# ReLU²-attention followed by a two-layer GELU block: a fourth batch's first layer in block form behind attention, and a new order of all operations

## The chip, the cores and the metric

One core of a Trainium2 chip. The time is the device time of one execution in microseconds (us); lower is better. Engines: PE (TensorE, matmuls), DVE (VectorE), ACT (ScalarE), POOL (GpSimd, which here mainly issues loads), SP (SyncE, which issues transposing transfers and stores).

## What is computed

Eight batches, twelve heads, 448 tokens, head size 64. All inputs and the output are float32; the kernel computes in bf16 with float32 sums.

```python
scores = (q @ k.T) / sqrt(64)                  # per batch and head
attn   = maximum(scores, 0)**2 / 448
x      = (attn @ v), heads side by side        # (8*448) x 768
h      = x @ w_in                              # 768 -> 2048
out    = gelu_exact(h) @ w_out                 # 2048 -> 768
```

## The kernel before

**Attention.** Batches 0 and 1 are transposed on PE. From batch 2 on, `add_load` issues one load for each four heads ("group") of k and q from POOL, casting to bf16, and one load `ldV` for a whole batch of v. `add_T_dma` then issues nine transposing transfers from SP (`turn`, L662): per group one for k (`kT`) and an even and an odd one for q (`qT`). A batch's q and k lie in one buffer, `nq` and `nk`, that all batches from 2 on share: a group of the next batch can only be loaded when this batch's transpositions of it are done. `add_gate` (L703) is a tiny POOL copy that reads a transposed tile; everything behind it in POOL's queue, the next loads above all, waits until that group's transpositions have landed. `qT` and `kT` have two buffers each, so batch b's transpositions also wait for the scores of batch b-2.

Per batch there are 21 score steps (`QK`, L736, four quadrant matmuls), each followed by a ReLU that empties PSUM (ACT L748 or DVE L750) and a square on DVE (L757), and three value products (`AV`, L797, 28 matmuls each) whose results are copied to `xT`.

**First layer.** In plain form (`add_f1`, L849) a batch takes 16 products of six matmuls of 448 columns, each followed by a GELU on ACT. In block form (`add_blocks`, `add_block`, L993) x and `w_in` are cut in 2x2 blocks and seven products of half-size blocks replace eight: 28 products of six matmuls of 224 columns, plus four sums of x blocks (L960), and, for each of four sub-blocks, one copy out of PSUM on ACT and five additions on DVE (L1030). The sums of weight blocks (`add_wsums`, L918) are made once; one of them overwrites a part of `win_sb`, so no plain product may come after it. Batches 0 to 4 are plain, batches 5 to 7 in block form.

**Second layer.** Tokens are taken in groups of 256 (`add_group`, L1166), seven products each, with sums and additions on DVE (L1147, L1200) and two stores from SP (L1127) out of three `osb` buffers. The first 256 tokens are done by `add_plain` (L1261).

**Order.** Every operation is an `Op` in one list, `sch.open`. `Scheduler.place` walks a string, `ORDER`, and issues the operations in that order: a letter names the engine (P PE, A ACT, D DVE, G POOL, S SP), the number is the operation's place in the list. `Z1056` is a filler: matmuls on zeros of 1056 columns (L1499). Each engine runs its own operations strictly in this order, so an operation that waits holds up all behind it on its engine. Between the attention steps PE runs "flow": plain first-layer products and second-layer groups; what belongs to `end` follows.

Of the kernel before, what the change touches and what calls it, by code (L numbers as in the profile page):

```python
# [26 lines left out]
KF = FF // 128  # L27
# [24 lines left out]
LEAD = 8  # L52
HALF_M = 6
# [30 lines left out]
G0 G1 G2 G3 G1435 G4 G5 G6 A10 P11 D13 A16 P17 G7 D12 P14 D18 P42 P39 G8 P19 A15 P21 D43 P33 P36 D44  # L84
A40 D20 Z128 A22 P54 G9 P25 P23 A37 D34 P51 D26 P48 A55 Z1056 D35 A24 P69 D56 Z1024 D41 A49
P57 Z992 D38 A52 P63 Z448 G117 D70 P45 A58 D53 P66 A64 D50 P27 A46 G118 P31 D59 P60 D28 A67
G119 D32 A47 P78 P29 D65 G120 A61 P81 Z1088 D68 D30 A79 P93 D62 P108 Z544 D71 A82 P84 Z992
G121 A94 P75 D109 P72 G122 D83 A85 P90 P129 D80 G123 D73 A76 P105 A74 P102 D95 G124 P131 D130
A91 P141 D86 A106 D77 P111 P96 D132 A103 P165 P143 D92 A112 D104 D107 A97 P156 D113 P87 G125
D98 A166 P99 D110 G126 D88 A157 P114 A142 D100 A89 P174 G127 A101 P168 D115 P133 A144 P135  # L90
A116 G128 D175 P171 P159 A169 D134 P251 D136 D170 A160 P145 D158 A172 D167 A252 P162 P186 D176
P192 P243 A146 D161 G147 D173 A187 G148 P253 D193 A163 A244 D164 P195 G149 P180 P198 P137 A254
G150 P139 D196 A181 P183 P177 G151 D138 A199 D140 A184 P189 P219 P245 D178 G152 A190 D185 P247
G153 D194 A220 D179 A246 G154 P213 D188 P222 P204 P263 D221 A248 G155 D197 A214 D200 P265 D191
A205 D182 A264 P261 A223 A266 P216 D224 S231 P207 P201 D206 A262 A208 S229 P210 P259 D209 A217
D215 S232 P255 D211 A260 P249 D212 D218 A256 D202 P225 A203 S228 A250 P257 S230 A226 P267 D227
A258 P348 S234 A268 P350 S233 A349 P352 G237 A351 G238 P354 S235 A353 G239 P288 S236 P294 P282
P358 A355 G240 G241 D289 P356 D283 A359 P360 D295 A357 D290 P306 P279 P276 D296 P362 A361 D307
P364 D280 A363 P366 D277 A365 P368 A367 P370 A369 P300 P285 P291 G242 P372 A371 G269 D286 A292
P374 G270 D284 A373 G271 P318 P303 D301 P312 G272 P376 D308 A375 G273 A304 D319 P378 D278 A377  # L100
P380 D313 A379 D293 G274 D314 D390 P382 D305 G275 D302 A381 D391 D287 D281 P330 P309 P297 S398
D392 A331 D320 P315 S399 P384 D393 A298 D396 A310 S401 A383 D417 P387 D394 D419 A385 D311 A299
D395 A316 D317 P324 P321 D418 A325 P333 D397 P327 A388 P421 D420 D322 S400 A328 D323 P423 D326
A334 D422 S386 P339 P336 P342 P425 D424 D329 A343 D335 P427 S402 A426 D337 P429 G407 A340 G408
S403 D428 P431 G409 D344 D338 S389 D341 P440 P437 D332 P345 S404 D430 A438 P443 D441 P446 S405
P433 D432 A346 D347 A444 P509 A447 D434 P511 D439 G410 D448 S406 A510 G411 P449 D442 P452 G412
P455 P513 D562 A512 S435 D445 S436 A453 P515 D454 A450 A514 P517 D456 D451 P464 D457 P461 P458
S541 A465 P467 D462 A518 P470 G413 S542 P519 A516 G414 A459 G415 P521 D471 S543 G416 D472 A520
P523 D466 A468 D460 S544 A522 P479 D560 P476 P473 D469 P525 A524 D463 A477 P527 D480 A474 D478
A526 P529 D475 D481 A528 P488 P485 P482 S545 A489 P494 D486 A530 P491 P531 D487 D483 P533 D495  # L110
A532 S546 P535 D496 A484 D561 A492 P503 D490 P500 A534 P497 D493 P537 A536 G550 G551 S547 P564
D498 G552 A538 D504 S548 P539 D499 A501 G553 A565 D505 P600 G554 D502 P603 P506 G555 S549 A601
P606 D604 A540 P609 P566 D563 A507 D602 P568 D607 D567 P570 D610 A569 A508 P572 D571 P624 P612
P618 S704 P574 D580 D608 A613 D573 P576 S705 G556 A619 D581 G557 D582 P627 S706 D575 P615 G558
P584 D614 G559 D577 S578 A616 D611 P586 S707 D605 A628 D617 A625 P636 D620 P630 S579 A585 P621
D629 G713 A631 D637 P633 G714 P588 D587 S708 G715 A622 D626 D623 A634 P639 P642 P648 D583 P590
D638 A640 D635 A589 D632 P592 D641 A643 D591 P651 A649 S709 D644 P657 P645 D593 A652 P666 D658
P654 P594 D653 A646 D659 A655 D650 P596 A647 D667 S710 D595 P660 P766 P663 P672 D597 A661 D767
P674 A664 S711 D662 A673 D656 P676 D668 A675 D665 P772 P769 P669 S712 G716 D773 A770 P763 S598
P775 A677 G717 P678 S599 D670 G718 A764 D771 P680 G719 D723 A776 S867 D768 A679 P790 P778 D765  # L120
A671 P781 G720 P682 A681 D777 G721 D791 P684 G722 S868 D725 A683 P686 D779 A782 A685 P688 D783
D780 D774 P787 P793 P784 D724 S869 A788 P799 D794 A687 P796 P690 A689 D795 D789 A797 P692 D798
A691 P694 A693 P696 A785 A695 S870 P698 A786 A800 P802 P811 A697 P805 D801 P700 A699 A803 D812
P702 S871 D792 A806 D804 P814 P817 D807 P808 A815 S872 P823 D818 A701 P820 P727 G876 D816 A703
G877 D809 S873 A821 G878 D726 P729 A810 D819 A728 D822 P826 D813 A824 P829 S874 P906 P731 D730
G879 A830 G880 D827 S875 P733 G881 A907 D828 D831 P912 D825 P921 P832 D745 A913 P909 A732 D922
P924 P735 D734 A833 A925 P737 A910 D743 A834 P936 D914 P918 P933 D736 P739 D738 S741 D744 A934
P747 D908 G882 A937 D740 G883 P749 D938 A919 S978 G884 D935 A748 G885 D926 P942 P930 S742 P915
P751 D750 A931 D943 S979 P753 D920 A916 A752 D746 P755 D923 S980 D911 D944 P948 P945 D917 P927
D888 A949 D754 P939 P757 D950 A928 D886 D756 P759 A946 D887 A940 D758 A929 P835 D932 D947 D941  # L130
S981 P957 P954 P951 A836 D958 A955 P960 P963 D760 P837 D959 A961 D952 P839 D956 A953 S982 A838
P966 D964 P972 P969 D962 P841 A840 S983 D889 A973 D965 P843 S984 A842 D967 P847 A970 S985 A844
P845 D971 D968 S761 D974 P990 P987 D1067 P975 S986 A991 P993 D988 A846 P996 S762 P849 D992
A848 D1068 A976 D1070 P851 A997 D989 A850 P853 A994 A977 D995 P1005 P1002 A852 P999 P855 A854
D1006 A1003 P859 D1004 A1000 D998 A856 P857 D1007 D1001 P1011 P1014 P1008 D1059 A858 A1012
P1017 D1015 P1026 P861 A1009 D1063 A860 P863 D1060 A1018 D1010 P1020 A1027 P1029 D1061 P1023
A862 P865 D1016 A864 D1019 P890 A1021 D1028 D1022 A866 P892 D1062 A1024 A891 D1013 P894 D1025
A1030 D1069 D893 P1035 D1031 P1038 P1032 D1064 A895 A1036 D1066 P1041 D1037 A1039 P1044 P896
D1033 A1042 D1034 D1040 P898 A1045 D1043 D897 P1047 D1046 P1050 P1053 P900 D899 A1048 D1139
P902 D1049 A1051 D1140 A1054 P1071 D1052 D1055 P1056 D901 S904 A1072 D903 S905 P1088 D1141  # L140
P1073 D1057 P1090 A1089 D1058 P1143 D1074 D1091 P1075 D1065 P1092 A1144 P1077 D1142 A1076
D1179 P1094 A1093 D1180 P1079 D1078 P1096 D1095 P1145 D1080 D1097 A1081 P1082 D1181 A1098
P1099 D1146 P1085 D1083 P1102 D1100 A1084 P1105 D1086 A1101 P1122 D1103 A1087 P1107 D1182
A1106 P1124 A1123 P1147 A1104 D1108 D1125 P1109 P1126 A1148 P1111 A1110 P1128 A1127 P1113
D1112 P1130 D1129 P1149 D1114 D1131 A1115 P1116 A1132 P1133 D1150 P1119 D1117 P1136 D1134
A1118 P1151 D1120 A1135 D1137 A1121 P1153 D1291 A1138 D1292 D1152 P1155 D1159 D1154 S1157
P1163 D1160 D1156 S1158 P1165 D1161 D1164 P1167 D1162 D1166 D1293 P1169 D1294 A1168 P1171
D1170 P1173 D1253 D1172 P1175 D1251 D1174 S1177 P1183 D1252 P1200 D1176 S1178 P1185 A1184
D1254 P1202 A1201 P1255 D1186 D1203 P1187 P1204 A1256 P1189 A1188 P1206 A1205 P1191 D1190
P1208 D1207 P1257 D1192 D1209 A1193 P1194 A1210 P1211 D1258 P1197 D1195 P1214 D1212 A1196  # L150
P1217 D1198 A1213 P1234 D1215 A1199 P1219 A1218 P1236 A1235 P1259 A1216 D1220 D1237 P1221
P1238 A1260 P1223 A1222 P1240 A1239 P1225 D1224 P1242 D1241 P1261 D1226 D1243 A1227 P1228
A1244 P1245 D1262 P1231 D1229 P1248 D1246 A1230 P1263 D1232 A1247 D1249 A1233 P1265 A1250
D1264 P1267 D1271 D1266 S1269 P1275 D1272 D1268 S1270 P1277 D1273 D1276 P1279 D1274 D1278
P1281 D1280 P1283 D1282 P1285 D1365 D1284 P1287 D1363 D1286 S1289 P1295 D1364 P1312 D1288
S1290 P1297 A1296 D1366 P1314 A1313 P1367 D1298 D1315 P1299 P1316 A1368 P1301 A1300 P1318
# [240 lines left out]
def kernel(  # L397
# [537 lines left out]
    def add_blocks(b):  # L935
# [34 lines left out]
        for m4 in (0, M1 // 2):  # L970
# [4 lines left out]
            for p in zip(*todo):  # L975
                atoms += [(0.58, o) for o in p]
# [445 lines left out]
    def at(b, n):  # L1422
        return [at_slot(b, n)]
# [112 lines left out]
```

## Time and profile before

| | |
|---|---|
| three runs, median (lowest, highest) | 370.13 us (369.83, 370.37) |
| profiled execution, first to last instruction (span) | 367.9 us |
| PE busy | 359.3 us, 98% |
| DVE, ACT, POOL busy | 285.1 (78%), 199.4 (54%), 62.9 (17%) us |
| HBM read, written | 45.61 MB, 11.01 MB |
| score steps of batch 7 on PE | 220.5 to 246.5 us |

The profiled execution has no other time than its span. The span goes from the first to the last instruction; the 2.2 us between it and the median lie around it, and are taken as the same before and after. "Busy" of PE is modelled, since matmuls overlap; how many microseconds a group of matmuls takes is read from the start of one group to the start of the next.

### The profile page before, as it was taken

What the parts mean: (1) busy time and instruction counts of PE and PEld (TensorE: products, weight loads), DVE (VectorE), ACT (ScalarE), POOL (GpSimd) and SP (SyncE); (2) the same over time, 40 slices, a digit from 0 to 9 for tenths busy, and PEclk for the clock granted to TensorE, in tenths of its full rate; (3) what the DMA queues carried; (4) which work ended last, traced back from release to release, by engine and by line L of the source; (5) the groups of instructions that cost most, each with busy time, mean ns of one, the idle gap of its engine ahead of it and who ended that gap; (6) DMA issues with size and microseconds to landing.
All of it is one profiled execution on the core that took longest, in us unless ns stands there. A gap on an engine that the chain in (4) does not pass through costs nothing.

```text
span 367.9 us, 8474 instructions
## 1 busy us (share of the span) xinstructions
PE 359.3 (98%) x3573; PEld 222.5 (60%) x3573; DVE 285.1 (78%) x473; ACT 199.4 (54%) x319; POOL 62.9 (17%) x103
## 2 busy tenths in 40 slices
PE   7999999999999999999999999999999999999995
PEld 6675654455544455544555544557876897688663
DVE  4998854699788889989598997998788558665862
ACT  5998954536367546765777568863540353045200
POOL 8766304230112140240302000000000000000000
PEclk9999999999999999999999999999999999999998
DMA  9999999999999999999999980002002301210233
GB/s 180 191 202 204 201 178 167 196 201 178 162 218 214 154 186 193 237 214 154 166 110 131 215 183 2 2 2 86 3 0 87 88 0 52 86 37 2 86 87 86
DMA packets 89542, 47.27 MB, mean 128 GB/s; under 512 B 55329, under 2 KB 86049, under 8 KB 89505
## 3 DMA queue, kind: packets, MB, share of 16 engines
q0 software_dynamic: 32912, 22.47, 43.8%
q1 hardware_dynamic: 55952, 23.76, 34.9%
q8 instruction: 28, 0.46, 0.5%
q10 hardware_dynamic: 640, 0.51, 0.4%
q14 instruction: 10, 0.07, 0.1%
HBM read 45.61 MB, written 11.01 MB: 154 GB/s over the span
## 4 chain that ended last, share of the span: by engine, by line
PE 78%; DMA 8%; SPq 5%; DVE 5%; issue 1%; POOL 1%; ACT 1%; DVEq 0%; POOLq 0%; ACTq 0%
PE pso L1166 30%; PE psh L849 19%; PE pb L993 13%; PE ps L736 8%; PE pav L797 7%; SPq L662 5%; DMA wout_sb<-in_moe_w_out_dram 4%; DVE a_sq L757 2%; DMA nq<-in_q_dram 1%; DVE t_sb L1103 1%; DMA qT<-nq 1%; DMA out_dram<-osb 1%; ACT a_sq L748 1%; PE tp L635 1%; DVE part L1030 1%
## 5 line engine op out<-in xcount | busy, mean ns | idle before, releaser
L748 ACT ACTIVATE a_sq<-ps 128x896 bf16<-128x896 f32 (+1 forms) x119 | 104.3, 918 | 36.8 <-PE ps L736 36.6
L757 DVE TENSOR_TENSOR a_sq<-a_sq 128x896 bf16<-128x896 bf16 (+1 forms) x169 | 97.0, 617 | 9.4 <-ACT a_sq L748 8.8
L849 PE MATMUL psh<-xT,win_sb 128*128 128x448 bf16 (+1 forms) x516 | 96.4, 340 | 0.4 <-issue 0.4
L849 PEld LDWEIGHTS <-win_sb 128*128 128x128 bf16 x516 | 48.1, 98 | 45.8 <-issue 9.7
L750 DVE TENSOR_SCALAR a_sq<-ps 128x896 bf16<-128x896 f32 (+1 forms) x50 | 53.5, 1078 | 17.1 <-PE ps L736 17.0
L859 ACT ACTIVATE h_sb<-psh 128x448 bf16<-128x448 f32 x80 | 43.2, 548 | 29.9 <-PE psh L849 29.6
L1166 PEld LDWEIGHTS <-s_sb 128*128 128x128 bf16 x424 | 40.7, 98 | 26.6 <-issue 2.0
L1030 DVE TENSOR_TENSOR part<-pb,part 128x448 f32<-128x448 f32 x60 | 34.6, 620 | 21.5 <-PE pb L993 21.5
L736 PE MATMUL ps<-qT,kT 64*64 64x448 bf16 (+1 forms) x756 | 47.9, 336 | 0.5 <-ACT a_sq L748 0.2
L1166 PEld LDWEIGHTS <-h_sb 128*128 128x128 bf16 x312 | 29.6, 98 | 22.5 <-issue 4.4
L1166 PE MATMUL pso<-wout_sb,s_sb 128*128 128x384 bf16 (+2 forms) x216 | 38.1, 320 | 0.1
L1166 PE MATMUL pso<-wout_sb,h_sb 128*128 128x384 bf16 x208 | 38.1, 326 | 0.0
L1166 PE MATMUL pso<-t_sb,s_sb 128*128 128x384 bf16 x208 | 38.1, 326 | 0.0
L797 PE MATMUL pav<-a_sq,v_sb 64*64 64x448 bf16 (+1 forms) x756 | 36.5, 329 | 0.3 <-issue 0.2
L736 PEld LDWEIGHTS <-kT 64*64 64x64 bf16 x756 | 18.5, 105 | 22.9 <-issue 17.1
L1039 ACT ACTIVATE h_sb<-part 128x448 bf16<-128x448 f32 x36 | 20.1, 578 | 20.2 <-DVE part L1030 19.9
L1200 DVE TENSOR_TENSOR osb<-pso,p_sb 128x384 f32<-128x384 f32 x39 | 21.7, 556 | 11.0 <-PE pso L1166 6.7
L993 PEld LDWEIGHTS <-win_sb 128*128 128x128 bf16 x288 | 27.6, 98 | 2.3 <-issue 0.4
L797 PEld LDWEIGHTS <-v_sb 64*64 64x64 bf16 x756 | 21.2, 107 | 11.7 <-issue 1.3
L703 POOL COPY gate<-qT 128x16 bf16<-128x16 bf16 x15 | 3.7, 246 | 111.0 <-DMA qT<-nq 111.0
L993 PEld LDWEIGHTS <-ws 128*128 128x128 bf16 x216 | 20.7, 98 | 0.0
L1147 DVE TENSOR_TENSOR s_sb<-h_sb 128x1024 bf16<-128x1024 bf16 x26 | 17.8, 685 | 2.3 <-PE pso L1166 2.3
(61 smaller groups left out, 298.4 us busy)
## 6 DMA issues: line engine op xcount, KB each, us to landing
nk<-in_k_dram POOLq DMA_DIRECT2D x23, 224.0 KB, 5.6
nq<-in_q_dram POOLq DMA_DIRECT2D x21, 224.0 KB, 8.3
v_sb<-in_v_dram POOLq DMA_DIRECT2D x5, 672.0 KB, 13.9
out_dram<-osb SPq DMA_DIRECT2D x8, 336.0 KB, 2.9
v_sb<-in_v_dram POOLq DMA_DIRECT2D x9, 224.0 KB, 8.6
out_dram<-osb SPq DMA_DIRECT2D x7, 288.0 KB, 3.2
out_dram<-osb SPq DMA_DIRECT2D x8, 240.0 KB, 3.0
win_sb<-in_moe_w_in_dram POOLq DMA_DIRECT2D x8, 192.0 KB, 8.6
```

Source lines behind the costliest of these rows:

```text
L736: nc.tensor.matmul(ps[64 * j : 64 * j + 64, e, x * w : x * w + w], kT[r, g, i * 128 + 64 * j : i * 128 + 64 * j + 64], moving, start=True, ...
L748: A.activation(ar, ps, AF.Relu, scale=c_att)
L750: V.tensor_scalar(ar, ps, c_att, 0.0, op0=mybir.AluOpType.mult, op1=mybir.AluOpType.max,)
L757: V.tensor_mul(box["a2"][:, :, :used], ar, ar)
L797: nc.tensor.matmul(pav[0][o2 : o2 + 64, e, :w], vt[b][r, 2 * g + e, bass.ts(i, D)], box["a2"][r, y, o : o + w], start=(i == 0), stop=(i == ...
L849: nc.tensor.matmul(ph[:, x * n : x * n + n], win_sb[:, kd, bass.ts(m + x, 128)], xT[b][:, kd, c], start=(kd == 0), stop=(kd == KD - 1),)
L859: A.activation(h_ring()[:, m : m + nm, o + c.start : o + c.stop], box[0][:, :S].rearrange("p (x n) -> p x n", x=nm), AF.Gelu,)
L993: nc.tensor.matmul(bank[name][:, y, z * HS : z * HS + HS], w[:, k, bass.ts(mm, 128)], right()[:, k], start=first and k == 0 and z == 0, st ...
L1030: V.tensor_add(get(to), ps(name), get(other))
L1039: A.activation(h_ring()[:, m : m + 2, o + half[c].start : o + half[c].stop], src().rearrange("p (x n) -> p x n", x=2), AF.Gelu,)
L1166: nc.tensor.matmul(box[bank][:, n0:n1], left()[:, kf], right()[:, kf, n0:n1], start=bool(need) and kf == 0, stop=kf == K2 - 1, skip_group_ ...
L1200: V.tensor_add(out()[:, n0:n1], box[bank][:, n0:n1], other()[:, n0:n1])
```

## The change

Batch 4 joins the batches in block form, so its 16 plain products leave attention's flow and 28 block products come behind it. The second-layer group 6 moves from batch 5's flow to batch 4's. Tiles for the x-block sums are dealt out differently (batch 6 takes the `qT` buffer, batch 7 waits for batch 4's products). `ORDER` is replaced as a whole; it has 1469 operations instead of 1436.

```diff
+NBLK = 4
 ...
-G0 G1 G2 G3 G1435 G4 G5 G6 A10 P11 D13 A16 P17 G7 D12 P14 D18 P42 P39 G8 P19 A15 P21 D43 P33 P36 D44
-A40 D20 Z128 A22 P54 G9 P25 P23 A37 D34 P51 D26 P48 A55 Z1056 D35 A24 P69 D56 Z1024 D41 A49
 ...
+G3 G4 G1468 G1 G0 G7 G118 A10 P11 D13 G117 A16 P17 D12 P14 G2 D18 P42 P39 G122 P25 D15 P23 A43
+G6 P33 D26 P36 A40 P21 G5 D24 P69 P19 A34 G9 P66 D37 P63 D22 A70 Z1216 D20 P57 A67 P48 D41 P29
 ...
@@ add_blocks
-                    tag = "qT" if b == B - 1 else "kT"
+                    tag = "qT" if b == B - 2 else "kT"
 ...
-        gone = [o for (bb, *_), o in QK.items() if bb == (B - 2 if b == B - 3 else B - 1)]
+        gone = [o for (bb, *_), o in QK.items() if bb == (B - 2 if b == B - NBLK else B - 1)]
+        if b == B - 1:
+            gone += first_blocks
 ...
-    F1B = {2: 1, 3: 2, 4: 3, 5: 4}
-    GROUPS = {2: (1,), 3: (2, 3), 4: (4, 5), 5: (6,)}
+    F1B = {2: 1, 3: 2, 4: 3}
+    GROUPS = {2: (1,), 3: (2, 3), 4: (4, 5, 6)}
 ...
-    add_wsums(at(B - 1, 1), [F1[B - 4, m, None] for m in range(KF)])
+    add_wsums(at(B - 1, 1), [F1[B - NBLK - 1, m, None] for m in range(KF)])
 ...
-    end = woven(add_blocks(B - 3), add_group(7))
+    end = add_blocks(B - 4)
+    end += woven(add_blocks(B - 3), add_group(7))
```

The two `ORDER` strings are too long to print. Counted out by the list of operations, they say this (K4.1: load of k, batch 4, group 1; V4: v of batch 4; kT, qE, qO: the transpositions of k, and the even and odd ones of q):

| | before | after |
|---|---|---|
| fillers (Z), columns | 8, together 6272 | 1, 1216 |
| PE runs, ahead of batch 3's first scores | six products of group 1, one AV and one score step of batch 2 | none of these; otherwise the same, fillers aside |
| PE runs, ahead of batch 4's first scores | F1 of batch 2, all 16 products; first product of group 2; AV of batch 3, groups 0 and 1 | seven of those 16; not that group product; AV of group 0 alone; one score step of batch 3 less; otherwise the same, fillers aside |
| PE runs, ahead of batch 7's first scores | groups 4 and 5 whole, seven products of batch 4's F1 | group 4's first four products; one AV and two score steps of batch 6 less |
| POOL's queue, batches 3 to 4 | gate 3.0, K4.0, Q4.0, gate 3.1, K4.1, Q4.1, gate 3.2, K4.2, Q4.2, V4 (V3 long before) | gate 3.1, gate 3.0, V3, Q4.0, gate 3.2, Q4.1, Q4.2, K4.2, K4.0, V4, K4.1 |
| POOL's queue, V of batch 2 | before `w_out` | V2.0 before `w_out`, V2.1 and V2.2 among batch 3's loads |
| SP's queue, batch 3 | kT0 qE0 kT1 qO0 (store) qE1 qO1 (store) kT2 qE2 qO2 | kT0 kT2 qO0 qE0 kT1 qE1 qO1 qO2 qE2 |
| SP's queue, batch 4 | two stores of group 1, then kT0 qE0 qO0 kT1 qE1 qO1 kT2 qE2 qO2 | qE0 qO2 kT0 qE2 (store) kT2 (store) qO0 qE1 kT1 qO1 |
| transpositions of batch 7 | kT0, store, qE0 qO0 kT1 qE1 qO1 kT2 qE2 (store) qO2 | kT0 (one store each of groups 3 and 2) qE2 qE0 qO2 kT2 qO0 (store) qO1 kT1 qE1 |
| block products | batch 5's begin just before the last AV; one batch after the other | batch 4's begin among batch 7's scores; those of batches 4, 5 and 6 overlap |

## The prediction

> **What bounds the kernel now.** I read the page's totals and slices first.
>
> ```profile
> span 367.9 us, 8474 instructions
> PE 359.3 (98%) x3573; PEld 222.5 (60%) x3573; DVE 285.1 (78%) x473; ACT 199.4 (54%) x319; POOL 62.9 (17%) x103
> ...
> DVE  4998854699788889989598997998788558665862
> ...
> DMA  9999999999999999999999980002002301210233
> ```
>
> PE's 98% is modelled, so it must be confirmed by starts; but the DMA row is full for the first 24 of 40 slices (220 us) too. Next the chain that ended last, in order of time:
>
> ```profile
> 111.62 1.32 PE pav L797 x28
> 112.94 0.38 PE ps L736 x8
> ...
> 173.30 5.78 PE psh L849 x30
> ...
> 259.46 4.60 PE pb L993 x48
> ...
> 341.24 22.14 PE pso L1166 x144
> ```
>
> From 102 us on it is PE almost alone. These rows give PE's prices, start to start: an AV 1.32, a score step 0.19, a plain product of six matmuls 1.135 (5.78 less 0.10 for the turn from attention's quadrant matmuls, over five), a block product 0.575 (4.60 over eight), a group product 1.30 (L1166, eight matmuls). Summing them over the old order gives 348.8 us, turns included; the last matmul ends at 363.4, so only 14.4 us are waits and start-up, nearly all of it in the first 33 us.
>
> Who keeps this going? The waits view has one large entry on POOL, and the gates are time stamps of when a group's transpositions have landed. Beside them I put the PE timeline at each batch's first score step.
>
> ```profile
> POOL gate L703 <- DMA qT<-nq: 111.0, 14, 16.7
> ```
> ```profile
> 96.74 0.21 POOL L703 COPY gate<-qT 128x16 bf16<-128x16 bf16 x1 [16.73 <-DMA qT<-nq]
> 125.36 0.24 POOL L703 COPY gate<-qT 128x16 bf16<-128x16 bf16 x1 [11.34 <-DMA qT<-nq]
> 148.25 0.73 POOL L703 COPY gate<-qT 128x16 bf16<-128x16 bf16 x1 [10.13 <-DMA qT<-nq]
> 177.67 0.21 POOL L703 COPY gate<-qT 128x16 bf16<-128x16 bf16 x1 [14.08 <-DMA qT<-nq]
> 180.28 0.21 POOL L703 COPY gate<-qT 128x16 bf16<-128x16 bf16 x1 [0.65 <-DMA qT<-nq]
> ```
> ```profile
> 100.64 0.57 PE L736 MATMUL ps<-qT,kT 64*64 64x448 bf16 x8
> 131.05 0.57 PE L736 MATMUL ps<-qT,kT 64*64 64x448 bf16 x8
> 156.90 0.76 PE L736 MATMUL ps<-qT,kT 64*64 64x448 bf16 x12
> ```
>
> Group 0 of batches 3, 4, 5 landed at 96.7, 125.4, 148.2; PE first used it at 100.6, 131.05 and 157.1 (second step of the last row). So the slack is 4, 6 and 9 us, and for batch 6 (177.7 to 187.4) 10. The transfers are nearly as much a bound as PE; they hide by less than ten microseconds.
>
> **The change, part by part.**
>
> *Block form of batch 4.* Out go 16 products of 1.135 (18.16 us), in come 28 of 0.575 (16.10): 2.06 us less on PE, whatever the order. DVE gets 20 additions of 0.62 (L1030: 34.6 us over 60) and four x sums of 0.50: 14.4 us. The copy and the GELUs on ACT: four more copies of 0.54. The weight sums are as before.
>
> *Fillers and turns.* 6272 columns become 1216: 2.1 us at 2400 columns per us. In the old start-up they lie where PE would else wait, so they are worth between 0 and 2.1. Turns: 91 instead of 92, 0.1. With all of it PE work is 344.5, so 4.3 less; if the fillers only become waits, 2.2 less. I take 4.3, since what decides below is an absolute time of the transfers.
>
> *Everything in attention is wanted earlier.* This is the change's largest part. Ahead of batch 4's first scores the new PE order lacks nine plain products (10.2 us), a group product (1.3), an AV (1.3), a score step (0.2), turns (0.2) and the fillers (2.1): 15.3 us. So PE wants batch 4's group 0 at 131.05 - 15.3 = 115.7, where it landed at 125.4. For batch 3 (six group products, an AV, a score step, fillers, 11.5) it is 89.1 against 96.7; for batch 5 141.9 against 148.2; batch 6 169.7 against 177.7; batch 7 195.5 against 210 (the landing of SP's third transposition of it), and the old transfers ran on to 220.
>
> *Can the transfers be as much earlier?* A load without transpositions beside it ran at 200 GB/s (4 to 44 us: 7.99 MB), 1.15 us for 224 KB and 3.44 for a V of 672 KB. A transposition costs 0.87 at best (three between the gates at 177.67 and 180.28) and 1.3 by SP's issues when it stands alone. Mixed, both are slower:
>
> ```profile
> DMA packets 6438, 2.51 MB, mean 157 GB/s; under 512 B 4916, under 2 KB 6388, under 8 KB 6437
> ```
>
> That row is not in the page but in the DMA view of 112 to 128 us. And of 82 to 92 us:
>
> ```profile
> kT<-nk SPq DMA_TRANSPOSE x2, 11.6
> ```
>
> a transposition issued while loads are queued took 11.6 us to land.
>
> Batch 3: the new queue has V3 (3.4 us) behind the transpositions instead of ahead, while V2.1 and V2.2, which now come among batch 3's loads, were ahead in the old queue too. So 96.7 - 3.4 = 93.3, against 89.1: 4.2 late. Batch 4: ahead of qO0, its sixth transposition now and third before, are the same loads (V3 and all of batch 4's K and Q), V4, three transpositions more (2.6 to 3.9) and one store of 384 KB less (0 to 1.9 at 200 GB/s; 1.3 taken). From the old row: 125.4 + 2.6..3.9 - 1.3 = 126.7 to 128. From the other side, nothing mixed: batch 3 at 93.3, three more transpositions to gate 3.1 at 97.2, 1.5 until V3 moves, then V3, six K and Q and V4 (13.8) to 112.5, and the last three transpositions and their landing (3.9 + 2) to 118.4. The old row was a mixed one (157 of 200 GB/s over 16 us, 3.4 us lost) and the new queue mixes less, so I take the middle, 123: a wait of 7.3 (2.7 to 12.3) at batch 4's first score step. It holds up all of PE, and includes batch 3's 4.2.
>
> What is late next: with PE 7.3 later, batch 5 is wanted at 149.2 and was there at 148.2; batch 6 at 177.0, there at 177.7; batch 7 at 202.8. There the old transfers lost about 5 us waiting for a gate and a store, three stores fewer save 3.9 at the same price, three transpositions more cost 2.6 to 3.9: 204 to 206. SP now also has a store of groups 3 and 2 each behind batch 7's kT0, with three `osb` buffers, and group 4's second addition needs one. 0 to 3 us more; I take 1.
>
> *DVE.* I lay its rows' means along the new PE order: from PE work 100 to 260 they come to 20.2 to 22.7 us for each 20, 21.4 on average (before 19.4). The nearest row is the old end of attention, 23.1 by the same sum:
>
> ```profile
> 230.00:250.00 20.00, 19.82 (x195) 10.55 (x193) 19.69 (x32) 14.57 (x21) 0.00 (x0) 1.00 0.01 2
> 350.00:367.90 17.90, 13.36 (x91) 8.36 (x88) 8.60 (x16) 0.00 (x0) 0.00 (x0) 0.94 0.31 89
> ```
>
> DVE 19.69 of 20, PE waiting 0.2. So the 14.4 us are covered; without cover 0 to 2. I take 0.
>
> *Sum.* 367.9 - 4.3 + 7.3 + 1.0 = 371.9 of span; with 2.2 around it 374.1.
>
> *Two rules of the skill.* The last row shows the clock at 0.94 where PE stands idle for 4.5 us at the end, the only such place. The Trainium skill ("TensorE: Matmul & The Clock Gate", HAM clock gate) says that an idle window of about 3.4 us halves PE's clock until about as long a busy one; a wait of 7.3 would cost up to 1.7 more, 375.8 in all, an estimate from that page. Of loads beside transpositions "DMA: Bandwidth & Descriptors" (Queues, rings and completion order) says that each DMA engine goes round its queues packet by packet; by it a transposition would come through a load's backlog at half pace, not the 11.6 us of the row, batch 4 would land at about 118 and the sum be 369. The row decides.
>
> **The rivals.**
>
> *The order holds (24 in 100).* The loads of batches 3 and 4 unmix so well that batch 4 lands before 117 and PE never waits. For it: the mixed row lost 3.4 us in 16, and the new queues have loads and transpositions more apart. Against: the DMA row has no empty slice to win. Time: 367.9 - 4.3 + 0 to 2 + 2.2 = 365.8 to 367.8, faster. It decides at a landing before about 119, where the wait falls under 4.3 less 0.7.
>
> *A wait as large as the gain (9).* Landing at 119 to 120.5: 369.4 to 370.9.
>
> *Waits add up (14).* The clock falls (an idle PE of over 4 us, twice, as at the end: 1.1 us lost in each), landing at 128 and batch 7 three late: 363.6 + 12.3 + 3 + 2.2 = 381.1, down to 378.
>
> *The change doesn't do what it says:* the 2.06 us could only fail if block products cost more than 0.575, and 84 of them in three batches didn't; under 1 in 100.
>
> **How the numbers follow.** The forecast, 370.9 to 378 with 374.1 likeliest, has 53. A measurement of this kernel can tell about 0.2% (0.74 us). Faster 0.24, same 0.09, slower 0.67. The range, 366.0 to 380.0, leaves out the bottom of the first rival and the top of the last, 0.1 together, and as much for what no case foresees; the forecast's own is 370.9 to 378.
>
> **What would show it.** Right: PE has its longest wait, 2.7 to 12, before score steps of batch 4 (with 4 before batch 3's), put down to `qT`; gate 4.0 after 118; block products at 0.575; after 250 us no new wait. Wrong: PE starts batch 4's scores before 117; or the wait is on `ps`/`osb` buffers, thus DVE's; or in the first 33 us PE loses more than before.

## The result and the profile after

The changed kernel takes 399.28 us (median of six runs, 397.39 to 401.04) against 369.98 us (369.55 to 370.38) for the kernel before on the same chip: a ratio of 1.0781, with a 95% interval of 1.0752 to 1.0810. It is slower, as forecast, but by 29 us where 4 were forecast, and outside the range.

The page of the changed kernel, totals and slices:

```profile
span 399.3 us, 8628 instructions
...
PE 364.3 (91%) x3632; PEld 231.4 (58%) x3632; DVE 299.5 (75%) x504; ACT 196.0 (49%) x316; POOL 63.4 (16%) x103
...
PEclk9999998999997799999899999999999999999999
DMA  9999999999999899799799720100200022220232
GB/s 173 199 202 197 178 163 164 203 194 170 177 184 168 121 152 166 137 199 174 118 176 164 166 65 21 61 2 1 80 2 1 2 80 79 80 79 2 70 90 79
```

PE has fallen from 98% to 91% of a longer span. The DMA row is still full to about 230 us; it has become no shorter, and its GB/s dip (121, 137, 118). And the clock row now has dips in the first half.

Its waits (us in total, times, longest), and PE in order of time around the longest:

```profile
POOL gate L704 <- DMA qT<-nq: 100.4, 9, 19.4
PE ps L737 <- DMA qT<-nq: 15.8, 4, 10.3
PE pb L1000 <- DVE part L1037: 5.0, 8, 0.9
```
```profile
121.36 0.38 PE L737 MATMUL ps<-qT,kT 64*64 64x448 bf16 x4
132.01 0.59 PE L737 MATMUL ps<-qT,kT 64*64 64x448 bf16 x4 [10.26 <-DMA qT<-nq]
132.35 2.86 PE L798 MATMUL pav<-a_sq,v_sb 64*64 64x448 bf16 x28
```

The kernel before had no row of PE waiting for `qT` at all. The second line is batch 4's first score step, 10.26 us idle; the first line is still a step of batch 3. The AV behind it takes 2.6 us to the next start instead of 1.32; PE's clock was low (0.75 over 115 to 135 us, below).

To see where the 31.4 us of the span went, I lay PE's starts in both traces along their orders and subtract the prices of the prediction (AV 1.32, plain product 1.135, block product 0.575, ...). What is left is start-up, waiting and slow matmuls (the sum of work comes out 1.2 us above the prediction's in both kernels, so the differences are not touched):

| up to | before: time, lost so far | after: time, lost so far | lost more than before | forecast |
|---|---|---|---|---|
| batch 3's first scores | 100.6, 11.4 | 95.2, 17.4 | 6.0 | 4.2 |
| batch 4's first scores | 131.0, 11.9 | 132.0, 28.1 | 16.2 | 7.3 |
| batch 6's first scores | 187.4, 12.3 | 188.0, 30.6 | 18.3 | 7.3 |
| batch 7's first scores | 220.5, 12.6 | 222.1, 39.2 | 26.7 | 8.3 |
| last matmul | 363.4, 13.4 | 394.7, 49.0 | 35.6 | 8.3 |

PE's work is 4.2 us less (forecast 4.3), so 35.6 - 4.2 = 31.4. The fourth line is the heart of it. Ahead of batch 7's first scores PE has 220.5 - 12.6 = 207.9 us of work before and 222.1 - 39.2 = 182.9 after: 25 us of work were taken away there, and the scores start 1.6 us *later*. All of the removed work, and a little more, turned into waiting; the same work, now behind attention, is paid in full, and 8.9 us of new waits come on top.

The first line hides something. At batch 3's first scores PE waits only 0.29 us. By batch 2's first scores about 2.5 us more had been lost than before, a little more than the 2.1 of fillers taken out, and 4.0 were lost at a score step of batch 2, by waiting and by slow matmuls behind it (the kernel before lost 0.8 of its own by then). PE in order of time, then the first 33 us before and after (columns as explained at the windows below; the second number is PE's busy time):

```profile
60.29 1.33 PE L737 MATMUL ps<-qT,kT 64*64 64x448 bf16 x12 [2.24 <-DMA qT<-nq]
```
```profile
0.00:33.00 33.00, 29.67 (x617) 22.17 (x621) 25.85 (x53) 26.46 (x41) 23.39 (x39) 1.00 1.25 193
0.00:33.00 33.00, 28.45 (x610) 21.89 (x611) 24.87 (x51) 26.85 (x41) 22.66 (x38) 1.00 1.24 190
```

Of the 8.4 us between batch 6's and batch 7's first scores 5.0 belong to batch 6's second group (3.6 of waiting and 1.4 of slow products) and 3.2 to batch 7:

```profile
193.46 0.59 PE L737 MATMUL ps<-qT,kT 64*64 64x448 bf16 x4 [3.59 <-DVE a_sq L758]
```

The profile puts this wait down to a square, but that ended at 192.96; this step also needs the group's even transposition, issued at 189.9 and landed at 193.4.

Who makes batch 7 late? The chain that ended last, and POOL in order of time, of the changed kernel:

```profile
203.01 0.83 POOL v_sb L567
203.83 13.19 DMA nk<-in_k_dram
217.04 1.64 SPq L663
218.78 3.19 DMA qT<-nq
222.10 0.57 PE ps L737 x8
```
```profile
99.18 0.47 POOL L704 COPY gate<-qT 128x16 bf16<-128x16 bf16 x2 [17.63 <-DMA qT<-nq]
...
162.99 0.63 POOL L704 COPY gate<-qT 128x16 bf16<-128x16 bf16 x1 [9.79 <-DMA qT<-nq]
...
194.47 0.48 POOL L704 COPY gate<-qT 128x16 bf16<-128x16 bf16 x2 [7.69 <-DMA qT<-nq]
195.09 0.73 POOL L470 DMA_DIRECT2D nq<-in_q_dram  x1
...
203.01 0.84 POOL L567 DMA_DIRECT2D v_sb<-in_v_dram  x1 [5.09 <-PE ps L737]
```

The gates are grouped: 3.1 and 3.0, then 5.0 and 5.1, then 6.0, 6.2 and 6.1 stand ahead of nearly all loads of the next batch, and in batches 5 and 6 one of them is that of the group whose transpositions SP issues last. So the loads of batch 6 start at 163.6, after the *last* transposition of batch 5 (landed 162.8), and those of batch 7 at 195.1, after the last of batch 6 (194.4). Loads and transpositions take turns. Before, a batch's loads started with the gate of its *first* group (148.2, 177.7) while the other groups were still being transposed.

The chain shows a second cause. V7 stands ahead of K7.2 and K7.1 in POOL's new queue, and it waited 5.09 us for PE: by the program it may only overwrite its buffer behind batch 5's last AV, which PE ran at 201.2. So K7.2 was issued at 203.8 and landed at 217.0; only then could SP issue the `kT` of that group, and `qO` of group 0 stands behind it. Before, V7 stands last.

The windows of the changed kernel (sum, PE, PEld, DVE, ACT, POOL busy, granted clock, DMA share, GB/s):

```profile
115.00:135.00 20.00, 9.74 (x79) 4.76 (x81) 7.14 (x11) 5.66 (x9) 0.91 (x2) 0.75 1.22 160
230.00:250.00 20.00, 19.74 (x205) 11.54 (x202) 19.69 (x34) 13.62 (x21) 0.00 (x0) 1.00 0.16 45
250.00:320.00 70.00, 64.12 (x602) 52.94 (x601) 53.63 (x98) 23.22 (x47) 0.00 (x0) 1.00 0.06 19
```

Behind 250 us DVE is busy 53.6 of 70 us, so it is not the bound, and yet PE stands still for up to 0.9 us again and again:

```profile
255.22 0.62 DVE L1037 TENSOR_TENSOR part<-pb,part 128x448 f32<-128x448 f32 x1 [2.08 <-PE pb L1000]
...
255.90 0.73 PE L1000 MATMUL pb<-xs,win_sb 128*128 128x224 bf16 x6 [0.71 <-DVE part L1037]
...
256.67 0.62 DVE L1037 TENSOR_TENSOR part<-pb,part 128x448 f32<-128x448 f32 x1 [0.30 <-PE pb L1000]
```

The addition at 255.22 reads the first half of a `pb` tile, whose product was done about 1 us earlier; it starts just when the product of the *other* half in that tile has ended (255.18), and in the string it stands behind that product. PE's next product needs the addition and waits for it.

### The profile page after: what moved, and what is told of

It reads as the page before. It is cut to its first block, busy times and chain, and to the rows that moved or that the text cites. A ratio compares the mean times of both kernels' runs of the same rounds, so it can differ in the third digit from the quotient of the medians.

```text
span 399.3 us, 8628 instructions
## 1 busy us (share of the span) xinstructions
PE 364.3 (91%) x3632; PEld 231.4 (58%) x3632; DVE 299.5 (75%) x504; ACT 196.0 (49%) x316; POOL 63.4 (16%) x103
## 4 chain that ended last, share of the span: by engine, by line
PE 50%; DMA 21%; SPq 10%; DVE 10%; issue 4%; ACT 2%; POOL 2%; DVEq 0%; POOLq 0%
PE pso L1173 19%; PE pb L1000 13%; SPq L663 9%; PE psh L850 8%; DMA v_sb<-in_v_dram 5%; PE pav L798 5%; DMA nq<-in_q_dram 5%; DMA qT<-nq 4%; PE ps L737 4%; DVE part L1037 4%; DMA nk<-in_k_dram 3%; DMA wout_sb<-in_moe_w_out_dram 3%; DVE a_sq L758 2%; ACT a_sq L749 2%; DVE a_sq L751 1%
## 5 line engine op out<-in xcount | busy, mean ns | idle before, releaser
L749 ACT ACTIVATE a_sq<-ps 128x896 bf16<-128x896 f32 (+1 forms) x121 | 105.7, 922 | 52.2 <-PE ps L737 52.2
L850 PE MATMUL psh<-xT,win_sb 128*128 128x448 bf16 (+1 forms) x420 | 80.0, 344 | 0.0
L751 DVE TENSOR_SCALAR a_sq<-ps 128x896 bf16<-128x896 f32 (+1 forms) x48 | 51.5, 1076 | 29.1 <-PE ps L737 28.8
L737 PE MATMUL ps<-qT,kT 64*64 64x448 bf16 (+1 forms) x756 | 49.4, 343 | 20.8 <-DMA qT<-nq 15.8
L1037 DVE TENSOR_TENSOR part<-pb,part 128x448 f32<-128x448 f32 x80 | 47.1, 618 | 23.3 <-PE pb L1000 22.9
L860 ACT ACTIVATE h_sb<-psh 128x448 bf16<-128x448 f32 x64 | 34.5, 548 | 27.8 <-PE psh L850 27.6
L1046 ACT ACTIVATE h_sb<-part 128x448 bf16<-128x448 f32 x48 | 25.5, 575 | 33.6 <-DVE part L1037 18.6
L1000 PEld LDWEIGHTS <-ws 128*128 128x128 bf16 x288 | 27.6, 98 | 3.0 <-issue 1.3
L516 ACT COPY part<-pb 128x448 f32<-128x448 f32 x16 | 8.2, 534 | 41.6 <-PE pb L1000 41.6
L1000 PE MATMUL pb<-xs,win_sb 128*128 128x224 bf16 x192 | 22.3, 259 | 3.2 <-DVE part L1037 2.6
## 6 DMA issues: line engine op xcount, KB each, us to landing
v_sb<-in_v_dram POOLq DMA_DIRECT2D x5, 672.0 KB, 11.6
```

Source lines behind the costliest of these rows:

```text
L737: nc.tensor.matmul(ps[64 * j : 64 * j + 64, e, x * w : x * w + w], kT[r, g, i * 128 + 64 * j : i * 128 + 64 * j + 64], moving, start=True, ...
L749: A.activation(ar, ps, AF.Relu, scale=c_att)
L751: V.tensor_scalar(ar, ps, c_att, 0.0, op0=mybir.AluOpType.mult, op1=mybir.AluOpType.max,)
L850: nc.tensor.matmul(ph[:, x * n : x * n + n], win_sb[:, kd, bass.ts(m + x, 128)], xT[b][:, kd, c], start=(kd == 0), stop=(kd == KD - 1),)
L860: A.activation(h_ring()[:, m : m + nm, o + c.start : o + c.stop], box[0][:, :S].rearrange("p (x n) -> p x n", x=nm), AF.Gelu,)
L1000: nc.tensor.matmul(bank[name][:, y, z * HS : z * HS + HS], w[:, k, bass.ts(mm, 128)], right()[:, k], start=first and k == 0 and z == 0, st ...
```

## The experiments

In all of them the order string, or a few lines, was edited; the names are those of the queues in the tables above. Ratios are to the kernel before on the same chip.

**The order inside SP's queue.**

```diff
 SP, batch 4
-qE0 qO2 kT0 qE2 (store) kT2 (store) qO0 qE1 kT1 qO1
+qE0 qO2 kT0 qO0 qE2 (store) kT2 (store) qE1 kT1 qO1
```

> The changed kernel with SP's queue alone altered for batch 4: qO0 stands directly behind kT0, ahead of qE2, two stores and kT2. In the changed kernel PE waits 10.5 us at the second score step of batch 4's group 0 (121.4 to 132.0 us) for qO0, issued at 128.1. Theory A (the order inside SP's queue made this wait): qO0 lands about four issues, some 4 to 5 us, earlier; the wait falls to about 5.3 and the time by about 5 us, to 394. Theory B (the transfers as a whole are too many for the time, whatever their order): batch 4's other groups and batches 6 and 7 then come as late as before against a PE that is 5 us ahead; waits of batches 6 and 7 (3.8 and 3.1 us now) grow by what batch 4's lost, and the time stays within 1 us of 399.

399.66 us, ratio 1.0777 (1.0706 to 1.0848). PE at batch 4's scores:

```profile
126.01 0.59 PE L735 MATMUL ps<-qT,kT 64*64 64x448 bf16 x4 [4.86 <-DMA qT<-nq]
...
137.92 0.59 PE L735 MATMUL ps<-qT,kT 64*64 64x448 bf16 x4 [3.11 <-DMA qT<-nq]
```

This is batch 4's first score step by PE's order, not its second. The wait fell from 10.3 to 4.9 us, as theory A has it, but the time did not follow: 3.1 us came back at the next group, and by batch 6's first scores PE had lost 29.8 us instead of 30.6. Theory B holds for the time. The longest wait is a symptom.

**Less to transfer.**

```diff
     def get_v(b):
+        if b > 2:
+            vt[b] = vt[2]
 ...
-            nc.gpsimd.dma_start(vt[b][:, 2 * g0 : 2 * g1], kv_view(v, b, g0, g1))
+            if b < 3:
+                nc.gpsimd.dma_start(vt[b][:, 2 * g0 : 2 * g1], kv_view(v, b, g0, g1))
```

> The changed kernel without the loads of v of batches 3 to 7; these batches multiply by v of batch 2, so their outputs differ from the reference. Five loads of 672 KB, 3.44 us each by the load row, are 17.2 us of transfers less, with all orders and all work of PE, DVE and ACT as they were. Theory B (volume of transfers): batch 4's wait of 10.5 us falls by the two V loads ahead of it (7 us) to about 3.5, the waits at batches 6 and 7 vanish, the clock stays up; time 384 to 387. Theory A (order of SP's queue, with its two stores ahead of qO0): the wait stays above 5 us; time 390 to 394. In both the waits among the block products (about 9 us behind 244 us) remain.

380.82 us, ratio 1.0276 (1.0225 to 1.0327). PE at batch 7's first scores:

```profile
201.33 0.57 PE L738 MATMUL ps<-qT,kT 64*64 64x448 bf16 x8
```

No wait stands there any more, and PE is 20.8 us earlier; it had lost 18.5 us by then instead of 39.2, hardly more than the 17.8 at batch 4's first scores. With the same work and orders, the time follows the loads: 17.2 us of them fewer made 18.5 us, theory B, and more than it expected (384 to 387). That the two numbers are so near is in part luck: without V7 its wait for PE, which held K7.2 up, is gone too (K7.2 issued at 180.0). What remains over the kernel before are the waits up to batch 3 and those behind attention.

**PE kept busy in its waits.**

```diff
 PE
-QK2.2.1 ... QK4.0.6 ... QK6.1.0 ... QK7.0.0
+Z4608 QK2.2.1 ... Z21504 QK4.0.6 ... Z7168 QK6.1.0 ... Z6144 QK7.0.0
```

> The changed kernel with matmuls on zeros put into PE's order where it waits: 4608 columns ahead of a score step of batch 2 (wait 2.3 us), 21504 ahead of batch 4's second score step (10.5), 7168 ahead of batch 6's second group (3.8) and 6144 ahead of batch 7's first scores (3.1). At 2400 columns per us each is a little shorter than the wait, so transfers and orders are as before and PE does not stand idle. Theory C (idle PE lowers the clock, which the changed kernel shows as 0.72 to 0.79 in the slices behind these waits): the slow matmuls behind each wait are gone, 4 to 5 us in all; time 394 to 395. Rival (what is slow behind the waits is transfers still landing, not the clock): time within 1 us of 399.

400.83 us, ratio 1.0807 (1.0757 to 1.0857).

```profile
115.00:135.00 20.00, 19.68 (x146) 9.55 (x145) 8.97 (x14) 7.78 (x13) 0.91 (x2) 1.00 1.17 175
```

The clock in this window went from 0.75 to 1.00 and the AV behind the wait from 2.6 to 1.32 us. So idle PE does lower the clock, as the Trainium skill ("TensorE: Matmul & The Clock Gate", HAM clock gate) has it. But nothing was won: batch 7's first scores start at 221.3 instead of 222.1, for the next transfer was waited for instead (3.4 us for the v of batch 5 at 175). Theory C had the mechanism right and its worth wrong: a slow matmul ahead of a wait costs nothing, nor did 16.4 us of needless matmuls.

**The old queues in the changed kernel.**

```diff
 POOL, batches 3 to 4 (5 to 7 alike)
-gate3.1 gate3.0 V3 Q4.0 gate3.2 Q4.1 Q4.2 K4.2 K4.0 V4 K4.1
+V3 gate3.0 K4.0 Q4.0 gate3.1 K4.1 Q4.1 gate3.2 K4.2 Q4.2 V4
 SP, batch 4 (3 and 5 to 7 alike; stores in their old slots)
-qE0 qO2 kT0 qE2 kT2 qO0 qE1 kT1 qO1
+kT0 qE0 qO0 kT1 qE1 qO1 kT2 qE2 qO2
```

> The changed kernel with the order of POOL's gates and loads and of SP's transpositions for batches 3 to 7 as in the kernel before: after each gate the two loads of its group, v last, transpositions group by group. In the changed kernel two or three gates stand ahead of nearly all loads of the next batch, and the first of them is that of a group whose transpositions come last (loads of batch 6 issued at 163.6 behind qE5.1's landing at 162.8, those of batch 7 at 195.1 behind 194.4), so that loads and transpositions take turns, 31 us for each batch, where the kernel before began the loads at the first group's landing and took 23 to 29. Theory E (the order of gates and loads makes the transfers late): batch 4 lands at 121 to 126, batch 7's first scores start at 206 to 212 instead of 222, time 383 to 389. Theory B (the amount of transfers alone): batch 7's first scores stay within 2 us of 222, time 397 to 401.

390.82 us, ratio 1.0536 (1.0458 to 1.0615): 8.5 us less than the changed kernel. First PE, then POOL:

```profile
97.25 0.96 PE L735 MATMUL ps<-qT,kT 64*64 64x448 bf16 x8 [5.25 <-DMA qT<-nq]
...
214.50 0.57 PE L735 MATMUL ps<-qT,kT 64*64 64x448 bf16 x8
```
```profile
180.25 0.21 POOL L702 COPY gate<-qT 128x16 bf16<-128x16 bf16 x1 [8.21 <-DMA qT<-nq]
180.78 0.70 POOL L547 DMA_DIRECT2D nk<-in_k_dram  x1 [0.33 <-issue]
```

The loads of batch 7 start right behind the first gate of batch 6, at 180.8 instead of 195.1, and its first scores at 214.5 instead of 222.1 without a wait: theory E, in the direction and most of the size. From batch 5's first scores to batch 7's PE lost 0.8 us (before the edit 9.3). But start and time were 2 us outside what was expected: in batches 3 and 4 the old queues gave some back, with 5.3 us at batch 3's first scores (v of batch 3 is ahead of its transpositions again) and 4.3 us at its last group, whose `qO` now landed at 115.0 instead of 100.6; batch 4's loads run beside it. Batch 4's `qO` of group 0 landed at 119.4 instead of 131.9 and PE did not wait for it, yet PE came to it at 132.3 as before: the waits had only moved to batch 3. POOL's and SP's orders were changed together, and V7 is last in its queue again; what the gates did and what V7's place did was not separated.

**The new queues in the kernel before.**

```diff
 POOL and SP, batches 3 to 7: the edit above, reversed, in the kernel before
```

> The kernel before with the changed kernel's order of POOL's gates and loads and of SP's transpositions for batches 3 to 7; PE, DVE, ACT, stores and the first layer as before. Theory F (the removed work ahead of each batch's scores is what uncovers the transfers; the new queues alone are just late enough to be hidden): batch 4 lands at 132 against 131 wanted, batches 5, 6 and 7 1 to 3 us after they are wanted; time 371 to 375. Theory E alone (the new queues by themselves make most of the loss): time 380 or more. Third: the queues are no worse than the old ones when PE is not early: 370.

376.42 us, ratio 1.0141 (1.0076 to 1.0206), 6.3 us over the kernel before.

```profile
175.20 2.83 PE L793 MATMUL pav<-a_sq,v_sb 64*64 64x448 bf16 x28 [4.46 <-DMA v_sb<-in_v_dram]
```

No score step waits for its transpositions; with the old work ahead of them the late queues are hidden, as theory F has it, though the time is 1.4 us above its 375. What it missed is v of batch 5, which the new queue puts behind three gates among batch 6's loads: landed at 175.2 instead of 147.6, 4.5 us of waiting and 2.0 of slow matmuls behind it. So the new queues cost 6.3 us here and 8.5 us in the changed kernel; the larger part of the loss stays when they are undone, and belongs to the work taken away and to the order behind attention.

**The block products in pairs.** The changed kernel up to batch 4's first block products, then this pattern:

```diff
 PE, each batch (x.0 and x.2: the two halves of one PSUM tile)
-p6.0 p5.0 p6.2 p7.0 p1.4 p7.2 ...
+p1.0 p1.2 p6.0 p6.2 p2.0 p2.2 p7.0 p7.2 p5.0 p5.2 p4.0 p4.2 p3.0 p3.2
```

> The changed kernel up to the first block products of batch 4; from there the block products stand in the pattern of the kernel before (both halves of one product next to each other, one batch after the other, groups 7 to 11 woven in). In the changed kernel the products behind attention wait about 9 us in sum, each time DVE's addition of one half starting only behind the product of the other half in the same PSUM tile. Theory D (this pairing of halves in time makes the waits): the 9 us go, less 4 to 8 us which DVE needs because batch 4's additions then have only their own products beside them; time 394 to 398, and the row of products waiting for additions changes from singles of 0.6 to 1.2 us to a DVE-bound stretch in batch 4 alone. Rival (DVE's total of additions is the bound behind attention whatever the order): time the same or up to 6 us longer.

418.38 us, ratio 1.1305 (1.1236 to 1.1373). Both theories missed it: 19 us worse than the changed kernel. Its waits:

```profile
PE pb L998 <- DVE part L1035: 17.8, 16, 1.4
```

PE's order was that of the kernel before for batches 5 to 7, where it has no such wait. The difference lay in the *interleaving* of the engines' words in the string. Here DVE's addition of the first half stood ahead of PE's product of the second half; before it stands behind it. No engine's own order differs by that. Two runs test that.

```diff
 order string, 19 places of the paired kernel, like
-P B5.0_p6  D B5.0_v2  P B5.2_p6
+P B5.0_p6  P B5.2_p6  D B5.0_v2
```

> The kernel of the paired block products (418 us) with 19 words of the order string moved and no engine's own order changed: each second half's product is issued ahead of the addition (or copy) that reads the first half of the same PSUM tile. In that kernel 18 of these products waited 0.8 to 1.6 us for the addition, 24 us in sum. Theory G (the program orders a product and an addition in the same tile by their place in the string, though they touch different halves): these waits go; time 394 to 399. Rival (DVE is too slow for the additions): time stays above 412.

396.48 us, ratio 1.0685 (1.0602 to 1.0768): 21.9 us faster than the paired kernel by 19 moved words. In its trace the products run through and the additions follow:

```profile
274.82 1.31 PE L998 MATMUL pb<-xs,ws 128*128 128x224 bf16 x12
275.02 2.30 DVE L1035 TENSOR_TENSOR part<-pb,part 128x448 f32<-128x448 f32 x4 [0.81 <-PE pb L998]
```

And the reverse in the kernel before:

```diff
 order string, 11 places of the kernel before, like
-P B6.0_p6  P B6.2_p6  P p1_g9  D B6.0_v2
+P B6.0_p6  D B6.0_v2  P B6.2_p6  P p1_g9
```

> The kernel before with no engine's own order changed; only the interleaving of the engines in the string: at 11 places of batches 5 to 7 DVE's addition of the first half stands ahead of PE's product of the second half in the same PSUM tile instead of behind it. Theory G: each place makes PE wait about 1.4 us as in the paired kernel; time 370 + 11 x 1.37 = 385. Rival (halves are independent, the string's interleaving is without effect): 370.

382.47 us, ratio 1.0309 (1.0247 to 1.0371). Its waits, and one of the places in order of time:

```profile
PE pb L988 <- DVE part L1025: 11.1, 11, 1.2
```
```profile
290.06 0.74 PE L988 MATMUL pb<-xs,ws 128*128 128x224 bf16 x6
...
290.91 0.62 DVE L1025 TENSOR_TENSOR part<-pb,part 128x448 f32<-128x448 f32 x1 [0.64 <-PE pb L988]
291.59 0.73 PE L988 MATMUL pb<-xs,ws 128*128 128x224 bf16 x6 [0.79 <-DVE part L1025]
```

Eleven places, eleven waits; 12.3 us, 1.1 each where 1.4 was expected (0.95 at the five `p6` places, 1.36 at the six `p5` ones, start to start). Theory G holds: this program orders a product and an addition in the same `pb` tile by their places in the string, though they touch different halves. The Trainium skill ("PSUM — Partial Sum Buffer", PSUM bank collisions raise a hardware error) has an error for two engines that touch the same bank and the same 32 partitions at once, and none where the banks differ. A bank is 2 KiB for each partition on that page, and each half of this tile is 512 floats, so by it the halves need not exclude each other. In this program the order kept for the tile as a whole makes them.

**Both mends together.** The edits of the old queues and of the re-issued pairs in one kernel.

> The changed kernel with both mended parts: old order of gates, loads and transpositions (391 us alone) and the block products in pairs with each product issued ahead of the addition of the other half (396.5 us alone). If the two causes are separate, their gains of 8.5 and 2.8 us add up: 386 to 390. If one covers the other (earlier batch 7 only moves into batch 4's DVE-bound stretch), 390 to 392. In both, the waits of 16 to 19 us ahead of batches 3 and 4's scores remain, so that it stays over the kernel before.

388.37 us, ratio 1.0498 (1.0463 to 1.0532): 399.28 - 8.5 - 2.8 = 388.0 was the sum. The two causes are separate. It still lost 27.5 us by batch 4's first scores (before: 11.9).

**The block form alone.** The kernel before up to 209 us of PE's order, then without batch 4's plain products:

```diff
 PE, behind F1_3 and group 5
-F1_4 (16 products) among the scores of batches 6 and 7
+scores and group 6 spread evenly; B4 (28 products, in pairs) behind the last AV
```

> Only the block form of batch 4, without the new order: the first 209 us of PE's order, all loads and transpositions are those of the kernel before; batch 4's 16 plain products are left out behind that, what remains of groups and scores is spread evenly, and 28 block products of batch 4 follow the last AV in pairs, then batches 5 to 7 as before. Theory H (the plain products were the work beside which batch 7's transfers and its squares on DVE ran; behind attention the block products stand alone beside their additions): batch 7's first scores start at 210 to 216, limited by landings at 205 to 213, and PE waits for squares at the end of attention; time 376 to 382 in spite of 2.06 us less PE work. Rival (block form pays as its sum of PE work says): 368 to 370.

380.80 us, ratio 1.0271 (1.0229 to 1.0313). The control, with three batches in block form and only the other engines' orders found anew behind that point:

> The kernel before, three batches in block form, PE's order unchanged, with the orders of the other engines behind 209 us found anew in the way that the two block runs above had them found. It shows what of their time is due to that alone: theory H expects 370 to 373, so that the difference to the block runs is the block form's; if it takes 376 or more, those runs say nothing on the block form.

373.83 us, ratio 1.0100 (1.0072 to 1.0128). So the block form, with the rest spread in this way, costs 7.0 us. That is not sharp: of the 9.0 us between the two profiled spans, 3.2 stand already at batch 6's first scores, where the orders do not differ yet, and 5.8 behind them. The windows of batch 7's scores, first of the block form, then of the control:

```profile
218.00:241.00 23.00, 19.44 (x217) 9.57 (x217) 23.00 (x39) 19.26 (x26) 0.00 (x0) 1.00 0.35 80
```
```profile
220.00:250.00 30.00, 29.64 (x284) 15.33 (x282) 26.77 (x42) 21.85 (x33) 0.00 (x0) 1.00 0.01 2
```

DVE is busy 23.00 of 23.00 us and sets the pace. By lines, in the first window:

```profile
L756 DVE TENSOR_TENSOR a_sq<-a_sq 128x896 bf16<-128x896 bf16 x21 | 12.1, 615 | 0.0
L917 DVE TENSOR_TENSOR ws<-win_sb 128x1536 bf16<-128x1536 bf16 x2 | 1.9, 950 | 0.0
```

Squares are 12.1 of the 23 us. The weight sums, four such rows, are 7.6, and they stand in the control's 30 us too. With the plain products gone the same work of DVE has less of PE's beside it. Theory H has the reason half right: squares, with the weight sums, yes; transfers, no, as no score step of it waits for `qT`, and batch 7 starts at 218.6, not 210 to 216. With groups 4 to 6 spread over a longer stretch:

```diff
 PE, from group 4 on
-groups 4 and 5 ahead of batch 7's scores, group 6 behind
+groups 4, 5 and 6 evenly among the scores of batches 6 and 7; B4's first two products ahead of AV7.2
```

> As the run above, but rearranged from 184 us of PE's order on: groups 4, 5 and 6 are spread evenly through the scores of batches 6 and 7, and two block products of batch 4 stand ahead of the last AV, so that more work is left for the end of attention. Theory H: a part of the waits for squares goes, batch 7's scores may come 2 us earlier; time 374 to 380, still over the kernel before. Rival: 366 to 369.

376.73 us, ratio 1.0181 (1.0166 to 1.0197), 2.9 us over the control (whose orders differ from the kernel before only behind 209 us, not 184).

```profile
213.00:239.00 26.00, 25.50 (x265) 12.66 (x264) 25.55 (x45) 21.37 (x29) 0.00 (x0) 1.00 0.31 84
```

PE and DVE are both nearly full, 25.5 of 26 us. This is the best of all kernels with four batches in block form; the kernel before stays the fastest.

## Why the prediction was wrong, step by step

*PE's work, 4.3 us less: right* (4.2 measured; a block product took 0.575 in the trace). But about as much as the fillers' 2.1 us of it was lost again in the start-up, a case that the prediction had named and not taken.

*Everything is wanted earlier: right, and it was the whole matter.* The step listed 11.5 to 25 us of work taken from ahead of batches 3 to 7: 25 us less work ahead of batch 7, and batch 7 started 1.6 us later. Batch 2 it did not look at; PE came to its scores earlier too and lost 4.0 us there.

*"Can the transfers be as much earlier?": the step that failed.* It asked the right question and answered it with landings that were too early.
- Batch 4's `qO0` was taken to land at 123, with bounds of 118.4 and 128. It landed at 131.9. "The new queue mixes less, so I take the middle" read loads and transpositions standing apart as a gain. The gain was not there: from 97 to 132 us the changed kernel moved 173 GB/s, the kernel before 187 (rows in the last section). PE, 6.0 us late by itself, waited 10.3 us there: 16.2 in sum instead of 7.3. Put ahead in SP's queue this transposition landed by 126.0, without v by 121.8, with the old queues at 119.4; in the first and the last of these the waits moved to other groups.
- Batch 7 was taken to land at 204 to 206 (its own terms give 203.7 to 205), 1 us late, and batch 6 was taken as no wait at all. Batch 7 landed at 222.0, and the two cost 8.4. The sum counted the bytes and SP's issues but not what stands in POOL's queue: two or three gates ahead of the loads of batches 6 and 7, and V7, which waits for PE, ahead of K7.2. With the old queues that part vanished.
- Batch 3 was taken to be 4.2 late. The 6.0 found there are near it by luck: 0.3 is batch 3's own wait, the rest start-up and batch 2.

*The volume.* "The transfers are nearly as much a bound as PE" was right, and stronger than said: 17.2 us of loads taken away gave 18.5 us of time (V7's hold on the queue went with them).

*DVE, 0 to 2 us: right for its throughput between 230 and 250 us (19.69 of 20, to the hundredth as before), wrong for its order.* "After 250 us no new wait" failed: 8.9 us of new waits lie behind batch 7's first scores, 5.0 of them put down by name to products that wait for additions. What makes such waits was shown in two other orders. In the changed one, pairs and re-issue together won back only 2.8 us; the trace then has 2.4 us of waiting for x sums in place of the 5.0. The prediction priced additions by their duration and never asked which product they stand behind in the string.

*The two rules.* The clock did fall behind the waits (0.75 in 115 to 135 us), but filling the wait moved no time, so the 1.7 us of the estimate were not owed. The page rule of packet by packet rounds ("DMA: Bandwidth & Descriptors", Queues, rings and completion order) would have had batch 4 at about 118; 131.9 speaks against reading a landing from it. Taking the row of 11.6 us was the better choice and still too kind: batch 4's first transposition took 10.9 us to land (111.1 to 122.0) and those behind it were issued 3.4 us apart.

*The rivals.* "Waits add up" (14 in 100, 378 to 381) had late batch 4 and late batch 7 right and was 18 us short; its low clock is there too, but costs nothing by itself. The rival on the other side asked for a landing before 119.

*The signs.* Longest wait before batch 4's scores, put down to `qT`: seen. Gate of that group after 118: seen. Wait of 4 us before batch 3's scores: not seen, 0.3. Block products at 0.575: seen. No new wait after 250: wrong. Of the signs of being wrong one was there: in the first 33 us PE stood still for 4.55 us instead of 3.33.

## What to carry to other kernels

Work that is taken out from beside a saturated transfer queue saves nothing there: it turns into waiting and is paid again where it was moved to, so compare, stage by stage, the work ahead of it with the landing of its data, and ask what makes the landing late. Read a queue with gates by what stands *behind* the gate: a gate on the last group ahead of the next batch's loads makes two transfers take turns, and unmixed is not faster if each waits for the other. A load that waits for a buffer holds up every load behind it. Where two engines use halves of one tile, look at the order in which the program issues them too: eleven places in the string, with no engine's own order changed, cost 12 us, and nineteen won 22.

## What the runs showed of the hardware that was not expected

A higher granted clock won nothing in a stage that waits for transfers: with the clock at 1.00 instead of 0.75 over 115 to 135 us the time was 400.8 against 399.3. Whether loads and transpositions run side by side or take turns does not by itself settle what the DMA engines move. Two windows each of the kernel before, of the changed kernel, and of the changed kernel with the old queues (the last number is GB/s):

```profile
97.00:132.00 35.00, 34.47 (x320) 17.33 (x321) 28.88 (x45) 20.52 (x33) 7.16 (x12) 1.00 1.29 187
130.00:200.00 70.00, 70.00 (x676) 36.34 (x675) 58.97 (x95) 46.40 (x71) 15.96 (x27) 1.00 1.23 171
```
```profile
97.00:132.00 35.00, 24.75 (x234) 12.56 (x227) 22.39 (x36) 17.80 (x26) 7.41 (x13) 0.90 1.19 173
130.00:200.00 70.00, 64.15 (x611) 32.29 (x612) 55.58 (x89) 41.49 (x62) 15.19 (x26) 0.94 1.02 152
```
```profile
97.00:132.00 35.00, 30.36 (x262) 15.07 (x262) 21.73 (x35) 18.72 (x27) 7.72 (x13) 0.86 1.27 155
130.00:200.00 70.00, 67.74 (x682) 34.50 (x681) 62.57 (x100) 46.63 (x71) 15.97 (x27) 1.00 1.30 171
```

In the later window, where batches 6 and 7 are loaded, taking turns moved less (152 against 171); in the earlier one the old queues moved the least. How much of this is mixing, how much waiting for gates and how much the order inside each queue was not separated. Also open is how to take the 16.2 us, 28.1 against 11.9 (27.5 with both mends), out of the stretch ahead of batch 4. Leaving out v took 10.3 of them away; the rest is start-up, batch 2 and batch 3.
